# Merging the two halves of one product chain, and a later clock for stores, in a kernel with a planned order

## Chip, core and metric

The kernel runs on one core of a Trainium2 chip. The metric is the device time of one execution in microseconds (us). A core has a matrix engine (TensorE; PE in the rows, its weight loads PEld), VectorE (DVE), ScalarE (ACT), GpSimd (POOL) and SyncE (SP). Here SP issues all loads and the stores of the result, and POOL issues the stores to scratch memory.

## What is computed

For each of 8 batches, memory attention over 8 heads of 576 tokens; the heads are joined to rows of 512 values, and two feed-forward networks follow (512 to 2048 to 512 each), the first with SiLU, the second with ELU.

```python
a = softmax(phi, axis=tokens)                  # 576 tokens, 32 memory slots
k_m, v_m = a.T @ k, a.T @ v                    # per batch and head
attn = softmax(q @ k_m.T / 8)
x = (attn @ v_m) joined over heads             # 4608 x 512
h = x @ moe_w_in;  x = (h * sigmoid(h)) @ moe_w_out
h = x @ moe2_w_in; out = elu(h) @ moe2_w_out
```

## The kernel before

**Stages.** A first part, to about 84 us, runs batch 0 in an order written out by hand (`FIRST`). From there to about 718 us `plan_first` runs the end of batch 0 and batches 1 to 6 and prepares all weights; then batch 7's last product and the whole second network (9 blocks of 512 tokens) follow under a second plan. The output of the first network goes to scratch memory (`x2d`) and is read back by the second.

**Numbers as two halves.** Operands of the large products are split into a high and a low fp16 part, after a scaling by a power of two taken from a sum of squares. The weights `w_out` of the first network (`w1o`) are read as four column blocks `wB[0..3]`. Blocks e and e + 2 belong to half e (0 or 1), each half with its own scale `s_w1o[:, e]`. `plan_w1o` waits for the sums of squares of its own two blocks, forms four sums of quarters (VectorE), splits seven operands j = 0..6 (high part on ScalarE, low part on VectorE, tile `hl_q`), and stores each to scratch (`w1os[e][j]`, POOL). `plan_quads` does the same for the second network's weights (`w2is`, `w2os`): a load into the buffer `raw`, five steps of conversion into `quad`, then splits and stores. `hl_q` lies in the same two `raw` buffers, so that a load waits for an earlier store to land, and a split too.

**Seven products in place of eight.** The second matrix product of the first network is computed from seven products of quarters (`plan_out1`): product j runs 8 steps over both halves e, alternating, into the PSUM pair `ph` (one bank for each half). The results are then copied (ScalarE, `copy_of`) or added (VectorE, `add_to`) into `y`, one instruction for each half: tile `y` is 4 x 288 values for one half, in two buffers (`NY`). After that the half is stored (`x2d`, POOL), and `squares` sums its squares in place on ScalarE, for the scale of the second network. That instruction overwrites `y`, so it waits until the store has landed.

**The plan.** `Plan` is a list scheduler that runs while the program is built. Each task has an engine, an estimated cost, a rank and dependencies; tasks are issued engine by engine, each time the ready task of the lowest rank at the earliest free time. In the plan of `plan_first` the ranks come from due times (`by_due`, with `ahead` = 35 us). The engines work through the resulting order and take no notice of the estimates: where an estimate was too short, an instruction waits in its place and holds all behind it on its engine. The estimates that matter here:

```python
def load(self, kb, ...):  cost = (2.2 if self.ahead is None else 3.6) + late + kb / 350
def store(self, kb, ...): cost = 4.0 + kb / 200, of which the POOL queue is held 1.2
t = pl.store(590, r - 2500, store, ...)          # plan_out1, one for each half
... pl.add("ACT", act(4 * HS), r - 100, squares, [t])
```

A load of 1024 KB is thus put at 6.5 us, a store of 512 KB at 6.56 us and a store of 590 KB at 6.95 us.

Of the kernel before, what the change touches and what calls it, by code (L numbers as in the profile page):

```python
# [39 lines left out]
NY = 2  # L40
NT = 3
KVLATE, QLATE = 1.0, 3.0
NKV = 3
# [47 lines left out]
def attn_moe_moe(ctx: ExitStack, tc: tile.TileContext, qT, phiT, kvm, kvt, w1i, w1o, w2i, w2o, out):  # L91
# [96 lines left out]
    class Plan:  # L188
# [62 lines left out]
        def run(self):  # L251
# [44 lines left out]
    s_w1o, n_w1o, p_w1o, q_w1o = col("s_w1o", 2), col("n_w1o", 2), col("p_w1o", 2), col("q_w1o", KD * NS)  # L296
# [53 lines left out]
    def junk_tile():  # L350
        return big.tile([P, 4 * HS], F32, tag="y", name="junk", bufs=NY).bitcast(F16)

# [97 lines left out]
    def plan_pair(pl, rank, e, s_all, n_all, negative, part, store, items, deps):  # L450
# [6 lines left out]
        for i, (get, j) in enumerate(items):  # L457
            s = (n_all if j in negative else s_all)[:, e:e + 1]
# [32 lines left out]
    def plan_w1o(pl, rank, e, ready, deps):  # L491


        def get():
            m, c = small("mq1"), kept("mq4", 4)
            for k, d in enumerate((e, e + 2)):
                nc.vector.tensor_copy(c[:, 2 * k:2 * k + 2], q_w1o[:, NS * d:NS * d + NS])
            nc.vector.tensor_reduce(out=m, in_=c, axis=AX.X, op=ALU.add)
            return m

        sc = plan_scales(pl, rank, e, get, s_w1o, n_w1o, p_w1o, ready)
# [15 lines left out]
        def pair(rank, items, deps):  # L517
            read, done = plan_pair(pl, rank, e, s_w1o, n_w1o, (3,), part_out, store_out(w1os), [
                (quad.get(x) or (lambda x=x: t[x]), j) for x, j in items], deps + [sc])
# [21 lines left out]
    def plan_quads(pl, due, src, e, shape, s_all, n_all, p_all, part, store):  # L541
# [43 lines left out]
        def pair(k, items, deps):  # L585
            pl.due = due[k]
            read, _ = plan_pair(pl, 0, e, s_all, n_all, (3,), part, store, [
# [135 lines left out]
    def mem_scales(b):  # L723

        z = st[b]
        z["inv1"], z["pvw"], z["c1"], z["io1"] = (kept(x, n, 3) for x, n in (("inv1", NF), ("pvw", 1), ("c1", 1), ("io1", 2)))
# [313 lines left out]
    def y_tile(name="y"):  # L1040
        return big.tile([P, 4, HS], F32, tag="y", name=name, bufs=NY)

# [13 lines left out]
    def plan_out1_first(pl, rank, ready):  # L1056
# [14 lines left out]
        def result(d):  # L1071
            z["x", d] = y_tile("x2e").rearrange("p a s -> p (a s)")[:, :S]
            acopy(halves(z["x", d]), z[d][0])

        for d in range(KD):
# [7 lines left out]
            c = pl.add("ACT", act(S, False), rank, lambda d=d: result(d), [t] + pl.ring("y", NY))  # L1083
            free.append(c)
            xfree = pl.take("y", c)
# [98 lines left out]
    def plan_out1(pl, b, r, silus, made, stored, scales, y_tile, y_ring):  # L1184
# [6 lines left out]
        w = [dict() for _ in range(2)]  # L1191
# [14 lines left out]
        def unit(e, j, q):  # L1206
            bank, at = BANK[j]
            if bank not in ps:
                ps[bank] = ps_half(SLOT[bank])[1]
            t = z["T", WSEQ.index(j)]  # L1210
            mm3([ps[bank][e]], [slice(0, HS)], [
# [28 lines left out]
        def copy_of(e, bank, s, deps):  # L1240
            def fn():
                if "y" not in w[e]:
                    w[e]["y"] = y_tile()
# [3 lines left out]
        def add_to(e, bank, s, from_, deps):  # L1247
            return pl.add("DVE", dve(HS), r - 2500, lambda: nc.vector.scalar_tensor_tensor(
                out=w[e]["y"][:, s], in0=ps[bank][e], scalar=z["io1"][:, e:e + 1], in1=w[e]["y"][:, from_],
                op0=ALU.mult, op1=ALU.add), deps)  # L1250

        E = range(2)
        C11, C12, C21, C22 = range(4)
        p1 = product(0, [])
        yfree = []
        c1 = []
        for e in E:
            c1.append(copy_of(e, 0, C11, p1 + [io] + pl.ring(*y_ring)))
            yfree.append(pl.take(y_ring[0], c1[e]))
        p2 = product(1, [])  # L1260
        c11 = [add_to(e, 1, C11, C11, [c1[e]] + p2) for e in E]
        p6 = product(5, c1)
        u2 = [copy_of(e, 0, C21, [c1[e]] + p6) for e in E]
        p7 = product(6, c11)
        s7 = [copy_of(e, 1, C22, [c1[e]] + p7) for e in E]
        p5 = product(4, u2)
        c22 = [add_to(e, 0, C22, C22, [s7[e]] + p5) for e in E]
        p4 = product(3, s7)
        c21 = [add_to(e, 1, C21, C21, [u2[e]] + p4) for e in E]
        p3 = product(2, c22)  # L1270
        c12 = [copy_of(e, 0, C12, [c1[e]] + p3) for e in E]
        free[0] += c12
        free[1] += c21
        done = []
        for e in E:
            def store(e=e):
                nc.gpsimd.dma_start(out=x2d[b][:, e::2], in_=w[e]["y"].rearrange("p (a t) s -> p a (t s)", a=2))
# [365 lines left out]
    def plan_first():  # L1643
# [84 lines left out]
        for b in range(1, B):  # L1728
# [24 lines left out]
            plan_out1(pl, b, 1000 * b + 400, silus, 0, stored if b == 1 else {}, [A[b]["scales"]], y_tile, ("y", NY))  # L1753
# [11 lines left out]
    with tc.manual_schedule():  # L1765
# [16 lines left out]
        for n in range(NT):  # L1782
            last["T_free", n] = pl.take("T", None)
        out1, loads = plan_out1(
            pl, B - 1, 0, None, NT, {}, [], lambda: ph2.tile([P, 4, HS], F32, tag="y", name="y", bufs=2), ("y", 2))
# [8 lines left out]
        for i in range(NB):  # L1794
# [3 lines left out]
            if i == 2:  # L1798
                pl.add("DVE", 2.5, 1000 * i + RANK["x2"], lambda: x2_scales(B - 1, NB), [y[i]["t_done", KQ - 1, 0]] + out1)
# [53 lines left out]
```

## Time and profile before

| | us |
|---|---|
| median of 3 runs | 1409.9 (1408.24 to 1411.55) |
| the profiled execution | 1407.48 |
| its span on the core | 1405.5 |
| PE busy | 1354.2 |
| DVE busy | 1127.9 |
| ACT busy | 951.1 |

A row of the timeline gives the start in us from the start of the span, the duration in us, the engine, the line of the kernel, the operation, its tiles and how many were merged into the row; in brackets stands the time that the engine sat idle before it and what released it. "PEclk" is the clock that the chip granted to TensorE, as a share of its full 2.4 GHz; the other level is 1.2 GHz. Ends of matmuls are modelled, so a busy PE need not be a fast one.

### The profile page before, as it was taken

What the parts mean: (1) busy time and instruction counts of PE and PEld (TensorE: products, weight loads), DVE (VectorE), ACT (ScalarE), POOL (GpSimd) and SP (SyncE); (2) the same over time, 40 slices, a digit from 0 to 9 for tenths busy, and PEclk for the clock granted to TensorE, in tenths of its full rate; (3) what the DMA queues carried; (4) which work ended last, traced back from release to release, by engine and by line L of the source; (5) the groups of instructions that cost most, each with busy time, mean ns of one, the idle gap of its engine ahead of it and who ended that gap; (6) DMA issues with size and microseconds to landing.
All of it is one profiled execution on the core that took longest, in us unless ns stands there. A gap on an engine that the chain in (4) does not pass through costs nothing.

```text
span 1405.5 us, 28627 instructions
## 1 busy us (share of the span) xinstructions
PE 1354.2 (96%) x12048; PEld 1092.9 (78%) x12048; DVE 1127.9 (80%) x1753; ACT 951.1 (68%) x1357; POOL 51.1 (4%) x85
## 2 busy tenths in 40 slices
PE   4999999999989999999998999999999999999998
PEld 2667676776756767676786888888888888888887
DVE  6889788796977989797767787887879787878784
ACT  3667765957857596776657576767667676767583
POOL 0001100000010010011000000000000000000000
PEclk8999999999999999999999999999999999999999
DMA  9565767367475657736293233332424151514130
GB/s 363 178 227 176 287 246 255 140 218 278 150 246 197 232 188 253 257 129 224 104 369 132 83 112 107 110 109 84 135 69 151 43 177 43 163 56 136 57 120 31
DMA packets 68801, 233.06 MB, mean 166 GB/s; under 512 B 9025, under 2 KB 15169, under 8 KB 64065
## 3 DMA queue, kind: packets, MB, share of 16 engines
q1 hardware_dynamic: 60288, 199.78, 42.1%
q0 software_dynamic: 8384, 31.46, 5.6%
q8 instruction: 94, 1.54, 0.4%
q14 instruction: 35, 0.28, 0.1%
HBM read 186.12 MB, written 40.89 MB: 162 GB/s over the span
## 4 chain that ended last, share of the span: by engine, by line
PE 79%; DMA 7%; DVE 4%; issue 4%; ACT 4%; POOL 0%; SPq 0%; ACTq 0%; POOLq 0%; DVEq 0%
PE ph L1020 24%; PE o L1020 22%; PE h2A L1020 12%; PE h2D L1020 9%; PE ph L1069 4%; DMA wi<-w2is 3%; PE ph L1027 2%; PE sc L775 2%; PE up L860 2%; PE kvp L679 1%; DMA kv<-in_kvm 1%; DMA x2d<-y 1%; DMA raw<-in_w2i 1%; DMA w2is<-hl_q 1%; DVE T L175 1%
## 5 line engine op out<-in xcount | busy, mean ns | idle before, releaser
L1020 PE MATMUL o<-t,wq 128*128 128x256 f16 x3024 | 361.4, 273 | 1.3 <-DVE t L175 1.3
L1020 PEld LDWEIGHTS <-wi 128*128 128x128 f16 x3024 | 296.2, 98 | 50.1 <-issue 7.2
L1020 PEld LDWEIGHTS <-wq 128*128 128x128 f16 x3024 | 296.1, 98 | 36.3 <-issue 1.7
L1020 PE MATMUL ph<-T,w1s 128*128 128x288 f16 x2352 | 301.9, 286 | 0.0
L1020 PEld LDWEIGHTS <-w1s 128*128 128x128 f16 x2352 | 225.9, 98 | 64.7 <-issue 8.6
L1020 PE MATMUL h2A<-xh,wi 128*128 128x256 f16 x1728 | 228.2, 274 | 10.0 <-ACT h L1457 6.0
L1457 ACT ACTIVATE h<-h2A,inv 128x256 f32<-128x256 f32 x288 | 133.3, 467 | 111.7 <-PE h2A L1020 108.9
L1020 PE MATMUL ph<-aT,u 128*128 128x288 f16 x1344 | 179.8, 290 | 8.8 <-ACT h L1106 8.5
L1020 PEld LDWEIGHTS <-u 128*128 128x128 f16 x1344 | 129.0, 99 | 59.2 <-issue 26.4
L170 ACT ACTIVATE t<-h,s_g 128x768 f16<-128x768 f32 (+1 forms) x144 | 147.4, 1037 | 37.5 <-DVE h L1499 25.9
L1020 PE MATMUL h2D<-xh,wi 128*128 128x256 f16 x1296 | 172.0, 274 | 0.1
L175 DVE SCALAR_TENSOR_TENSOR t<-h,s_g,t 128x768 f16<-128x768 f32 (+1 forms) x144 | 163.4, 1145 | 4.9 <-ACT t L170 4.9
L175 DVE SCALAR_TENSOR_TENSOR T<-h,c,T 128x1152 f16<-128x1152 f32 x98 | 137.2, 1412 | 22.7 <-ACT T L170 22.6
L1461 DVE SCALAR_TENSOR_TENSOR h<-h2D,inv,h 128x256 f32<-128x256 f32 x216 | 102.4, 480 | 65.1 <-PE h2D L1020 43.8
L170 ACT ACTIVATE T<-h,c 128x1152 f16<-128x1152 f32 x98 | 119.9, 1253 | 25.1 <-DVE h L134 19.9
L134 DVE TENSOR_TENSOR h<-h 128x256 f32<-128x256 f32 (+1 forms) x302 | 128.5, 463 | 3.0
L1499 DVE SCALAR_TENSOR_TENSOR h<-e,h 128x1024 f32<-128x1024 f32 x72 | 87.9, 1221 | 20.7 <-ACT e L1495 20.2
L1106 ACT ACTIVATE h<-ph,inv 128x576 f32<-128x576 f32 x112 | 82.1, 737 | 15.9 <-PE ph L1020 15.4
L1492 ACT ACTIVATE e<-h 128x1024 f32<-128x1024 f32 x72 | 75.5, 1048 | 13.7 <-DVE h L1461 13.6
L1495 ACT ACTIVATE e<-e 128x1024 f32<-128x1024 f32 x72 | 75.7, 1051 | 1.0
L1069 PE MATMUL ph<-h,w1o 128*128 128x288 f32 x256 | 66.7, 416 | 0.0
L134 DVE TENSOR_TENSOR h<-h,h 128x1152 f32<-128x1152 f32 x42 | 56.5, 1353 | 7.2 <-ACT h L1106 7.0
(183 smaller groups left out, 1271.2 us busy)
## 6 DMA issues: line engine op xcount, KB each, us to landing
w1s<-w1os SPq DMA_DIRECT2D x98, 512.0 KB, 4.5
wi<-w2is SPq DMA_DIRECT2D x56, 896.0 KB, 4.7
kv<-in_kvm SPq DMA_DIRECT2D x48, 256.0 KB, 5.5
q<-in_qT SPq DMA_DIRECT2D x32, 288.0 KB, 7.3
out<-ye SPq DMA_DIRECT2D x36, 256.0 KB, 2.0
raw<-in_w1i SPq DMA_DIRECT2D x8, 1024.0 KB, 11.5
raw<-in_w1o SPq DMA_DIRECT2D x8, 1024.0 KB, 4.9
raw<-in_w2i SPq DMA_DIRECT2D x8, 1024.0 KB, 6.7
```

Source lines behind the costliest of these rows:

```text
L134: nc.vector.tensor_tensor(out=out, in0=a, in1=b, op=op)
L170: nc.scalar.activation(out=hi, in_=x, func=AF.Copy, scale=s)
L175: nc.vector.scalar_tensor_tensor(out=lo, in0=x, scalar=s, in1=hi, op0=ALU.mult, op1=ALU.subtract)
L775: nc.tensor.matmul(ps[o:o + 64, c // 2, 2 * p:2 * p + 2], z["q", p][:, t0:t0 + 64], z["kT"][:, p // 2, 64 * (p % 2):64 * (p % 2) + 64], st ...
L1020: nc.tensor.matmul(o, w, x[:, c], start=first, stop=last, **how)
L1069: nc.tensor.matmul(z[d][1][t], wB[d][:, k], h[k // KQ][:, t, k % KQ], start=(k == 0), stop=(k == KF - 1))
L1106: nc.scalar.activation(out=h[m // KQ][:, :, m % KQ], in_=w.pop(m), func=AF.Silu, scale=z["inv1"][:, m // 4:m // 4 + 1])
L1457: nc.scalar.activation(out=w["x"][:, s], in_=w["A"], func=AF.Copy, scale=inv)
L1461: return pl.add("DVE", COST["add"], base, lambda: nc.vector.scalar_tensor_tensor(out=w["x"][:, s], in0=w["D"], scalar=inv, in1=w["x"][:, s ...
L1492: nc.scalar.activation(out=w["e"], in_=w["x"][:, B21:], func=AF.Relu, scale=-1.0)
L1495: nc.scalar.activation(out=w["e"], in_=w["e"], func=AF.Exp, scale=-1.0)
L1499: nc.vector.scalar_tensor_tensor(out=x, in0=w["e"], scalar=-1.0, in1=x, op0=ALU.add, op1=ALU.max)
```

## The change

There are five parts. (1) One scale for the whole of `w_out`: its columns become single, and `plan_w1o` for both halves waits for one `plan_w1o_scales`, which needs the sums of squares of all four blocks. (2) `y` becomes one tile for both halves in one buffer, and `copy_of`, `add_to` and `squares` each become one instruction over both halves; the two stores remain. The first batch's `x2e` uses quarters of the same tile. (3) `squares` gets rank 0 in `plan_first` (where due times replace it) and rank 1200 for the last batch, which puts it after ScalarE's work on the second network's first block (`in2`); and the gate that opens the second network's PSUM buffers no longer waits for it. (4) In `plan_first` a store is estimated 2 us longer and a weight load into `raw` (`plan_quads`) 2 us longer. (5) There ScalarE and VectorE may stay free for up to 0.6 us, where the chosen task would end over 0.3 us after a task arrives whose rank is lower by more than 10.

```diff
-NY = 2
+RAWLATE, STORE = 2.0, 6.0
+SOON, EARLIER = 0.6, 10.0
...
-            return self.add("POOL", 4.0 + kb / 200, rank, fn, deps, 1.2)
+            return self.add("POOL", (4.0 if self.ahead is None else STORE) + kb / 200, rank, fn, deps, 1.2)
...
                     i = min((i for i in r if at[i] <= start), key=lambda i: (self.tasks[i][2], i))
+                    if self.ahead is not None and eng in ("ACT", "DVE"):
+                        rank, end = self.tasks[i][2], start + self.tasks[i][1]
+                        soon = [k for k in r if start < at[k] <= start + SOON and end > at[k] + SOON / 2 and self.tasks[k][2] < rank - EARLIER]
+                        if soon:
+                            i = min(soon, key=lambda k: (at[k], k))
+                            start = at[i]
...
-    def plan_w1o(pl, rank, e, ready, deps):
+    def plan_w1o_scales(pl, rank, ready):
         def get():
-            m, c = small("mq1"), kept("mq4", 4)
-            for k, d in enumerate((e, e + 2)):
-                nc.vector.tensor_copy(c[:, 2 * k:2 * k + 2], q_w1o[:, NS * d:NS * d + NS])
-            nc.vector.tensor_reduce(out=m, in_=c, axis=AX.X, op=ALU.add)
+            m = small("mq1")
+            nc.vector.tensor_reduce(out=m, in_=q_w1o, axis=AX.X, op=ALU.add)
             return m
-        sc = plan_scales(pl, rank, e, get, s_w1o, n_w1o, p_w1o, ready)
+        return plan_scales(pl, rank, 0, get, s_w1o, n_w1o, p_w1o, ready)
+
+    def plan_w1o(pl, rank, e, sc):
...
-            load = pl.load(1024, 0, lambda k=k: load64(src, e, k), pl.ring("raw", 2))
+            load = pl.load(1024, 0, lambda k=k: load64(src, e, k), pl.ring("raw", 2), RAWLATE)
...
-        return big.tile([P, 4, HS], F32, tag="y", name=name, bufs=NY)
+        return big.tile([P, 2, 4, HS], F32, tag="y", name=name)
...
-        def copy_of(e, bank, s, deps):
+        def copy_of(bank, s, deps):
...
-                acopy(w[e]["y"][:, s], ps[bank][e], z["io1"][:, e:e + 1])
-            return pl.add("ACT", act(HS), r - 2500, fn, deps)
+                acopy(w["y"][:, :, s], ps[bank], z["io1"])
+            return pl.add("ACT", act(S), r - 2500, fn, deps)
...
-            def squares(e=e):
-                sumsq(mx_x2[:, b, e:e + 1], w[e]["y"], w[e]["y"])
-            t = pl.store(590, r - 2500, store, [c11[e], c12[e], c21[e], c22[e]])
-            yfree[e].append(pl.add("ACT", act(4 * HS), r - 100, squares, [t]))
-            done += [yfree[e][-1], c12[e], c21[e], p3[e]]
-        return done, [loads[j][0] for j in WSEQ]
+        def squares():
+            x = w["y"].rearrange("p e a s -> p (e a s)")
+            sumsq(mx_x2[:, b, 0:1], x, x)
+        t = [pl.store(590, r - 2500, lambda e=e: store(e), [c11, c12, c21, c22]) for e in range(2)]
+        yfree.append(pl.add("ACT", act(8 * HS), squares_rank, squares, t))
+        return p3 + [c12, c21], yfree[-1:], [loads[j][0] for j in WSEQ]
...
+        sc = plan_w1o_scales(pl, 260, sum(sq.values(), []))
         for e in range(2):
-            t, r = plan_w1o(pl, 260 + 20 * e, e, sq[e] + sq[e + 2], [])
+            t, r = plan_w1o(pl, 260 + 20 * e, e, sc)
...
-            pl, B - 1, 0, None, NT, {}, [], lambda: ph2.tile([P, 4, HS], F32, tag="y", name="y", bufs=2), ("y", 2))
+            pl, B - 1, 0, None, NT, {}, [], lambda: ph2.tile([P, 2, 4, HS], F32, tag="y", name="y"), ("y", 1), 1200)
```

## Rows read from the trace of the kernel before

**Rows 1.** Page, engines: busy us, share of the span, instructions.

```profile
PE 1354.2 (96%) x12048; PEld 1092.9 (78%) x12048; DVE 1127.9 (80%) x1753; ACT 951.1 (68%) x1357; POOL 51.1 (4%) x85
```

**Rows 2.** Windows: PE, PEld, DVE, ACT, POOL busy; clock; DMA; GB/s.

```profile
158.00:681.00 523.00, 511.22 (x4775) 373.27 (x4776) 429.64 (x583) 370.72 (x537) 38.75 (x57) 0.99 0.61 214
...
718.00:1405.50 687.50, 671.40 (x6083) 595.38 (x6080) 538.99 (x908) 467.64 (x653) 1.80 (x3) 1.00 0.33 108
```

**Rows 3.** Waits of PE over the span: total, times, longest us.

```profile
PE ph L1020 <- ACT h L1106: 8.5, 6, 4.3
PE h2A L1020 <- ACT h L1457: 6.0, 5, 3.9
```

**Rows 4.** Windows around four stalls of PE, columns as in rows 2.

```profile
100.00:116.00 16.00, 12.93 (x115) 9.31 (x104) 13.71 (x23) 9.32 (x19) 1.22 (x1) 0.89 0.86 254
328.00:350.00 22.00, 18.59 (x160) 12.11 (x159) 14.67 (x16) 15.79 (x24) 0.00 (x0) 0.92 0.75 271
400.00:433.00 33.00, 28.69 (x249) 18.14 (x248) 20.90 (x24) 22.47 (x32) 5.69 (x8) 0.90 0.70 235
736.00:772.00 36.00, 29.36 (x230) 23.81 (x228) 26.17 (x44) 26.77 (x38) 0.00 (x0) 0.91 0.43 151
```

**Rows 5.** Chain of waits, 310 to 331: start us, us, what.

```profile
310.27 2.48 DVE hl_q L175 x2
...
317.64 7.22 DMA w2is<-hl_q
325.05 6.19 DMA raw<-in_w2i
```

**Rows 6.** Timeline 331 to 334, with the idle time before.

```profile
331.27 1.12 ACT L311 ACTIVATE quad<-raw 128x1024 f32<-128x1024 f32 x1 [3.11 <-DMA raw<-in_w2i]
...
333.07 4.77 PE L1020 MATMUL ph<-aT,u 128*128 128x288 f16 x24 [2.02 <-ACT h L1106]
```

**Rows 7.** Timeline 399 to 418, the second stall of that kind.

```profile
399.87 1.28 DVE L175 SCALAR_TENSOR_TENSOR hl_q<-quad,s_w2i,hl_q 128x1024 f16<-128x1024 f32 x1
...
406.67 0.72 POOL L448 DMA_DIRECT2D w2is<-hl_q  x1 [5.30 <-issue]
...
415.57 1.15 ACT L170 ACTIVATE hl_q<-quad,s_w2i 128x1024 f16<-128x1024 f32 x1 [4.23 <-DMA w2is<-hl_q]
...
417.40 3.04 PE L1020 MATMUL ph<-aT,u 128*128 128x288 f16 x12 [4.27 <-ACT h L1106]
```

**Rows 8.** Timeline 729 to 744, the last batch's stores and squares.

```profile
729.45 1.43 POOL L1277 DMA_DIRECT2D x2d<-y  x2 [41.01 <-ACT y L178]
...
738.75 1.16 ACT L354 ACTIVATE y<-y 128x1152 f32<-128x1152 f32 x1 [3.00 <-DMA x2d<-y]
...
741.38 1.16 ACT L354 ACTIVATE y<-y 128x1152 f32<-128x1152 f32 x1 [1.38 <-DMA x2d<-y]
...
743.41 1.44 PE L1020 MATMUL h2A<-xh,wi 128*128 128x256 f16 x6 [3.88 <-ACT h L1457]
```

**Rows 9.** Lines by form: count, busy us, mean ns; copies, adds, SiLU.

```profile
L178 ACT ACTIVATE y<-ph,io 128x288 f32<-128x288 f32 x56 | 24.9, 495 | 29.7 <-PE ph L1020 28.2 <-DVE io L735 1.4
...
L1248 DVE SCALAR_TENSOR_TENSOR y<-ph,io,y 128x288 f32<-128x288 f32 x42 | 19.8, 509 | 2.7 <-PE ph L1020 2.6
...
L1106 ACT ACTIVATE h<-ph,inv 128x576 f32<-128x576 f32 x112 | 82.1, 737 | 15.9 <-PE ph L1020 15.4
```

**Rows 10.** Timeline at 150: the second scale of w_out is done.

```profile
150.19 0.15 DVE L488 TENSOR_SCALAR n_w1o<-s_w1o 128x1 f32<-128x1 f32 x1
```

**Rows 11.** DVE in the next 75 us, columns as in rows 2.

```profile
150.00:175.00 25.00, 25.00 (x220) 17.52 (x220) 19.30 (x19) 19.96 (x28) 4.29 (x8) 1.00 0.87 305
175.00:200.00 25.00, 25.00 (x222) 18.72 (x221) 21.44 (x20) 19.44 (x26) 0.53 (x1) 1.00 0.76 271
```

**Rows 12.** DMA issues: count, KB, median us to landing.

```profile
w1os<-hl_q POOLq DMA_DIRECT2D x14, 512.0 KB, 4.8
w2is<-hl_q POOLq DMA_DIRECT2D x14, 512.0 KB, 5.2
```

More of the change, by code (lines that the diff above doesn't have):

```diff
@@ L448, in store_in, with plan_pair @@
         nc.gpsimd.dma_start(out=w2is[e][:, :, j], in_=hl.rearrange("p (q c) -> p q c", q=4))
-    def plan_pair(pl, rank, e, s_all, n_all, negative, part, store, items, deps):
+    def plan_pair(pl, rank, e, s_all, n_all, negative, part, store, c, items, deps):
         z = {}
@@ L517, in pair @@
         def pair(rank, items, deps):
-            read, done = plan_pair(pl, rank, e, s_w1o, n_w1o, (3,), part_out, store_out(w1os), [
+            read, done = plan_pair(pl, rank, e, s_w1o, n_w1o, (3,), part_out, store_out(w1os), 0, [
                 (quad.get(x) or (lambda x=x: t[x]), j) for x, j in items], deps + [sc])
@@ L586, in pair @@
             pl.due = due[k]
-            read, _ = plan_pair(pl, 0, e, s_all, n_all, (3,), part, store, [
+            read, _ = plan_pair(pl, 0, e, s_all, n_all, (3,), part, store, e, [
                 (lambda x=x: t[x], j) for x, j in items], deps)
@@ L1082, in plan_out1_first @@
                 done[d, q] = t
-            c = pl.add("ACT", act(S, False), rank, lambda d=d: result(d), [t] + pl.ring("y", NY))
+            c = pl.add("ACT", act(S, False), rank, lambda d=d: result(d), [t] + (pl.ring("y", 1) if d == 0 else [done["y"]]))
             free.append(c)
-            xfree = pl.take("y", c)
+            if d == 0:
+                done["y"] = c
+                xfree = pl.take("y", c)
             t = pl.store(295, rank, lambda d=d: nc.gpsimd.dma_start(out=x2d[0][:, d], in_=z["x", d]), [c])
@@ L1182, in plan_w1s, with plan_out1 @@
         return t
-    def plan_out1(pl, b, r, silus, made, stored, scales, y_tile, y_ring):
+    def plan_out1(pl, b, r, silus, made, stored, scales, y_tile, y_ring, squares_rank=0):
         z = st[b]
-        w = [dict() for _ in range(2)]
+        w = {}
         ps = {}
@@ L1238, in product @@
             return [units(j, e, q, deps) for q in range(KQ) for e in range(2)][-2:]
-        def copy_of(e, bank, s, deps):
+        def copy_of(bank, s, deps):
             def fn():
-                if "y" not in w[e]:
-                    w[e]["y"] = y_tile()
-                acopy(w[e]["y"][:, s], ps[bank][e], z["io1"][:, e:e + 1])
-            return pl.add("ACT", act(HS), r - 2500, fn, deps)
-        def add_to(e, bank, s, from_, deps):
-            return pl.add("DVE", dve(HS), r - 2500, lambda: nc.vector.scalar_tensor_tensor(
-                out=w[e]["y"][:, s], in0=ps[bank][e], scalar=z["io1"][:, e:e + 1], in1=w[e]["y"][:, from_],
+                if "y" not in w:
+                    w["y"] = y_tile()
+                acopy(w["y"][:, :, s], ps[bank], z["io1"])
+            return pl.add("ACT", act(S), r - 2500, fn, deps)
@@ L1250, in add_to @@
+        def add_to(bank, s, from_, deps):
+            return pl.add("DVE", dve(S), r - 2500, lambda: nc.vector.scalar_tensor_tensor(
+                out=w["y"][:, :, s], in0=ps[bank], scalar=z["io1"], in1=w["y"][:, :, from_],
                 op0=ALU.mult, op1=ALU.add), deps)
-        E = range(2)
         C11, C12, C21, C22 = range(4)
         p1 = product(0, [])
[L1255 to L1259, printed above, removed]
@@ L1260, in plan_out1 @@
-        p2 = product(1, [])
[L1261 to L1271, printed above, removed]
@@ L1285, in plan_out1 @@
-        return done, [loads[j][0] for j in WSEQ]
+        c1 = copy_of(0, C11, p1 + [io] + pl.ring(*y_ring))
+        yfree = pl.take(y_ring[0], c1)
+        p2 = product(1, [])
+        c11 = add_to(1, C11, C11, [c1] + p2)
+        p6 = product(5, [c1])
+        u2 = copy_of(0, C21, [c1] + p6)
+        p7 = product(6, [c11])
+        s7 = copy_of(1, C22, [c1] + p7)
+        p5 = product(4, [u2])
+        c22 = add_to(0, C22, C22, [s7] + p5)
+        p4 = product(3, [s7])
+        c21 = add_to(1, C21, C21, [u2] + p4)
@@ new lines, in plan_out1, with store @@
+        p3 = product(2, [c22])
+        c12 = copy_of(0, C12, [c1] + p3)
+        free[0].append(c12)
+        free[1].append(c21)
+        def store(e):
+            nc.gpsimd.dma_start(out=x2d[b][:, e::2], in_=w["y"][:, e].rearrange("p (a t) s -> p a (t s)", a=2))
+        def squares():
[3 more added lines that the diff above has]
+        yfree.append(pl.add("ACT", act(8 * HS), squares_rank, squares, t))
@@ L1752, in plan_first @@
             U[b + 1] = plan_u(pl, b + 1, 1000 * b + 150, mem[b + 1], ready)
-            plan_out1(pl, b, 1000 * b + 400, silus, 0, stored if b == 1 else {}, [A[b]["scales"]], y_tile, ("y", NY))
+            plan_out1(pl, b, 1000 * b + 400, silus, 0, stored if b == 1 else {}, [A[b]["scales"]], y_tile, ("y", 1))
         n = 2
@@ L1783, in attn_moe_moe @@
             last["T_free", n] = pl.take("T", None)
[L1784 to L1785 removed]
+        out1, squares, loads = plan_out1(
+            pl, B - 1, 0, None, NT, {}, [], lambda: ph2.tile([P, 2, 4, HS], F32, tag="y", name="y"), ("y", 1), 1200)
         w1s_load = pl.gates["x"] = loads[4:5]
@@ L1798, in attn_moe_moe @@
             if i == 2:
-                pl.add("DVE", 2.5, 1000 * i + RANK["x2"], lambda: x2_scales(B - 1, NB), [y[i]["t_done", KQ - 1, 0]] + out1)
+                pl.add("DVE", 2.5, 1000 * i + RANK["x2"], lambda: x2_scales(B - 1, NB), [y[i]["t_done", KQ - 1, 0]] + squares)
             if i + 1 < NB:
```

22 lines of the change are left out of this document (9 added, 13 removed).

## The prediction

> **What bounds the kernel now.** Start with the page's list of engines: TensorE is busy for 96% of the span, VectorE for 80%, ScalarE for 68% [rows 1]. TensorE is the bound, and no part of the change takes a matmul away. So an instruction saved on ScalarE or VectorE is worth nothing by itself; what can be won is time in which TensorE stands still, or runs at the lower of its two clocks (1.2 for 2.4 GHz) after it stood still. Next come windows by stage: in the planned stage from 158 to 681 TensorE lacks 523 - 511.2 = 11.8 us, in the last one, from 718 on, 687.5 - 671.4 = 16.1 us [rows 2]. Then the waits of TensorE. The two large entries behind the opening are waits for ScalarE: 8.5 us for SiLU results of the first network (L1106) and 6.0 us for copies of the second (L1457) [rows 3]. ScalarE is idle for a third of the time, so these are not a lack of throughput: something stood ahead of the needed instruction. Windows around the places show what one such stall costs. The reader takes two things from each row: window less busy time, and one less the granted clock, times the window. At 328 that is 3.4 + 1.8 = 5.2 us, at 400 it is 4.3 + 3.3 = 7.6 us, at 736 it is 6.6 + 3.2 = 9.9 us, at 100 it is 3.1 + 1.8 = 4.8 us [rows 4]. The clock's share falls partly into the idle time, so these are upper ends.
>
> The chain of waits tells what stood ahead at 328. VectorE has finished the low part of a w2 operand at 310.27 + 2.48 = 312.75; the store that frees the buffer starts at 317.64 and lands at 324.86; the next weight load then takes 6.19 us [rows 5]. ScalarE waits 3.11 us for this load, with the SiLU that TensorE needs queued behind, and TensorE loses 2.02 us at once [rows 6]. The 24 matmuls after it take 4.77 us. The plan had put that store at 4.0 + 512/200 = 6.56 us; from data to landing it took 12.1, so it was 5.5 us late. The load was put at 6.5 us and took 6.2: it was not late by itself. At 415 it is the same with a store alone. Data are ready at 399.87 + 1.28 = 401.15, POOL cannot issue before 406.67 although it sits idle for 5.30 us, and ScalarE gets the buffer at 415.57, after an idle 4.23 us; TensorE then stands for 4.27 us [rows 7]. The third place is the change of networks: the last batch's stores are issued at 729.45, the squares of `y` wait for them, 3.00 and then 1.38 us, and TensorE stands for 3.88 us because the copies of the second network are queued behind [rows 8].
>
> **Part by part.**
>
> *Squares of the last batch (rank 1200).* In the old plan they had the lowest rank of all, so they went ahead of every copy as soon as the stores were thought landed (6.95 us). Now they come after ScalarE's work on the first block. The plan still fills a gap: if ScalarE is free and nothing else is ready, the squares go in, and may still wait. They now wait for both stores at once, the second of which let ScalarE go at 741.38 [rows 8]. Bounds: all of the 9.9 us of the place; or, if the gap comes at once, nothing. Below nothing too: one instruction over 2304 values takes about 2 x 1.16 = 2.3 us in one piece (estimate from rows 8), during which no copy can pass, so +2. I take -6, nearest to the wait itself (3.88) and its share of clock: at least most of the 4.4 us that ScalarE idled goes, since the copies that were ready then come first.
>
> *Stores and loads in `raw` planned 2 us later.* At 328 the chain of store and load gets 4 us more where it was 5.5 us late; the 3.11 us of waiting on ScalarE should be gone. I take the whole place, -5.2. At 400 only the store is in the chain: 2 of 4.23 us go, so I take 2.0/4.23 of 7.6 = -3.6. Together -8.8, rounded to -8 since the clock's share is an upper end. Bounds: 0 (the tasks that move into the space wait in their turn) and -12.8 (both places whole). Loads and stores that follow on SP and POOL are also issued later; their cover is that the plan works 35 us ahead of TensorE. Where that cover is gone, the price is a stall like the one at 100.
>
> A rule of the Trainium skill speaks against this part: "DMA: Bandwidth & Descriptors", section on the anatomy of one DMA on the GpSimd path, gives about 2.0 us plus the bytes at 436 GB/s, which for 512 KB is an estimate of 3.2 us. By it 6.56 us was ample already, and the sum would lose the -8. The rows differ: 4.8 and 5.2 us are the medians from issue to landing [rows 12], and the store of rows 5 took 7.2 us and waited 4.9 us for its issue.
>
> *One instruction for both halves.* 28 copies replace 56 and 21 adds replace 42. The copies go from 24.9 us of ScalarE to 28 x 0.737 (SiLU over the same 576 values) = 20.6; the adds cost 19.8 us now, and I leave VectorE's gain at about 2.5 (between 0 and half) [rows 9]. No product starts later, since it waited for both halves before. Nearly all of this lies beside TensorE's work. Only at the end of a batch does TensorE wait for a freed bank; there the pair is some 0.15 us shorter, seven times: -0.5 taken, bounds 0 and -2. The single buffer of `y` costs nothing: in the old form a half also waited for its own squares of the batch before, and these have most of a batch of room (seven batches lie between 158 and 718, 80 us each).
>
> *One scale for w_out.* Half 1's scale was there at 150.19 [rows 10]; the common one needs the same last sum of squares, so it comes then too. Half 0's work, done before that time until now, moves behind it: seven low parts of 1.28 us and four sums of the same shape, 11 x 1.28 = 14.1 us of VectorE, and 7 x 1.15 = 8 us of ScalarE [rows 7]. From 150 to 200 VectorE is idle for 50 - 19.3 - 21.4 = 9.3 us [rows 11], so 4.8 us do not fit and push other work. TensorE is busy for the full 50 us there, and the plan has 35 us in hand; that is the cover, and I take 0. Bounds: 0 and, with the cover gone, +14.1, plus 1.8 for the clock. Queued behind on POOL: the fourteen stores of 4.8 us median [rows 12] now come together, and behind them on SP the loads of these operands.
>
> *Waiting for urgent tasks.* A wait of up to 0.6 us puts a SiLU or a copy ahead of a split of 1.15 to 1.28 us. If the urgent task is late, the engine idles for nothing; VectorE is 82% busy from 158 to 681 [rows 2]. Everything behind 84 us is ordered anew by this and the other parts, and a new order has stalls of its own which no row of this trace can place. The nearest row is the stall at 100, where ScalarE waits for a load that was planned as it is now: 4.8 us [rows 4]. I take +4 for it all, between -5 (that stall goes, and none comes) and +10 (two such).
>
> **Sum.** -6 - 8 - 0.5 + 0 + 4 = -10.5 us. The profiled execution took 1407.5 us with a span of 1405.5, so it would come to 1397.0; it lies 2.4 us below the median of 1409.9, and on the median's scale I predict 1399.4.
>
> **Rivals.**
>
> (1) *The late stores stay late.* POOL waits with an idle engine for a store ahead of it (5.30 us in rows 7); the delay comes from the queue, not from the estimate, so a store behind another remains 3 to 5 us late and ScalarE waits elsewhere. For it: of fourteen stores most were within 6.56 us at the median, and still two pairs stalled. The rule of the Trainium skill on the page named above would end here too. Then -6 - 0.5 + 4 and -1 of the -8: 1406.4; without new stalls 1402.4. I put it at 1404. Chance 0.2.
>
> (2) *The squares only change their gap.* ScalarE has small gaps in the first block, the plan puts the 2.3 us into the first one past its 6.95 us, and the landing is just as late. Then the -6 shrinks to -1, and the sum is -5.5: 1404.4. Chance 0.12.
>
> (3) *Slower: the common scale of w_out.* Place: 150 to 230, the first use of the stored operands. VectorE's 14.1 us and the fourteen stores in a row hold the first products' weights, and TensorE waits for them in an order that cannot be changed any more. At the whole price of 15.9 us, with -6 - 8 - 0.5 + 4 beside it, the time is 1415.3. It decides the sign from the point where more than 10.5 us of the 15.9 land on TensorE. Against it: TensorE is busy throughout there, and the due times rank these splits first. Chance 0.13, with other slow new orders.
>
> (4) *No effect in sum*: gains and new stalls cancel, within 0.2% of 1409.9. Chance 0.1, beside the forecast's 0.45.
>
> **Range and chances.** A measurement of this kernel can tell about 0.2% (2.8 us) from no change. The forecast's own range, by the bounds, is 1390 to 1404; rivals 1 and 2 reach to 1406, the cancelled case to 1412, and only the slow case beyond that, with some of the forecast's lower end, is left out: 1390 to 1412. Faster: 0.45 + 0.18 + 0.1 = 0.73; within 0.2%: 0.1 + 0.04 = 0.14; slower: 0.13.
>
> **What would show it.** In the changed profile: no wait of ScalarE for `x2d<-y` with TensorE idle behind it, around 740, and the window there with a clock near 1.00; the squares as 7 instructions of about 2.1 us; 28 copies near 0.74 us; no wait of ScalarE for `raw<-in_w2i` or `w2is<-hl_q` over 2 us; half 0's stores of w_out after 150 and no wait of TensorE between 150 and 240. The prediction is wrong if stalls of TensorE on L1106 in the planned stage add up to as much as the 8.5 us of now, if the first use of `w1s` waits for a load, or if TensorE's stall at the change of networks stays above 3 us.

## Result: faster by 1.3%, and the profile after

The changed kernel takes 1391.0 us (median of 4 runs, 1390.5 to 1392.2), the kernel before beside it 1409.5. The ratio is 0.9869 with a 95% interval of 0.9852 to 0.9886: 18.5 us less, between 16 and 21. The prediction was 1399.4 with a range of 1390 to 1412. The direction and the range held; the size was 10.5 us by the forecast and is 18.5 by the medians, or 16.5 between the two profiled executions (1407.48 and 1390.94), whose spans are 1405.5 and 1389.2 us. One execution of a later kernel (the urgent wait limited to 0.5 us) took 5309 us for a reason that its record does not show, and is in no ratio below.

The page's engine line answers [rows 1]:

```profile
PE 1345.7 (97%) x12048; PEld 1089.7 (78%) x12048; DVE 1122.9 (81%) x1721; ACT 943.9 (68%) x1315; POOL 52.8 (4%) x84
```

TensorE has the same 12048 matmuls and is busy 1354.2 - 1345.7 = 8.5 us less. Equal work that takes less time is clock, and the mean granted clock, 0.989 before and 0.995 now, says the same: the share that is missing to 1 is worth about 15.5 us of the one span and 6.9 of the other. The rest of the 16.3 us of span, 7.8, is idle time that went. So about half of what these stalls cost lay in the lower clock that followed them.

Windows of the changed kernel at the places of [rows 4] (columns as there; the last one is moved by the 11 us that were won by then):

```profile
100.00:116.00 16.00, 12.85 (x122) 9.40 (x111) 12.03 (x18) 7.32 (x12) 0.35 (x1) 0.89 0.96 282
328.00:350.00 22.00, 21.84 (x202) 15.24 (x201) 16.66 (x17) 18.86 (x26) 0.00 (x0) 1.00 0.70 262
400.00:433.00 33.00, 32.31 (x298) 21.85 (x297) 27.01 (x29) 29.30 (x38) 5.68 (x8) 1.00 0.72 245
725.00:761.00 36.00, 32.64 (x286) 27.38 (x284) 30.44 (x50) 31.58 (x44) 0.00 (x0) 1.00 0.50 174
```

Idle time plus lost clock was 5.2, 7.6 and 9.9 us at the last three; it is 0.2, 0.7 and 3.4 now, all at full clock. The place at 100 stayed as it was (4.9 for 4.8). TensorE's waits over the span, answering [rows 3] (total, times, longest):

```profile
PE h2A L1029 <- DMA wi<-w2is: 6.9, 9, 2.0
...
PE kvTp L753 <- ACT pad L179: 4.1, 3, 3.2
PE ph L1029 <- ACT h L1119: 3.3, 7, 0.9
PE h2A L1029 <- ACT h L1466: 1.8, 5, 0.6
PE kvp L688 <- ACT quad L319: 1.5, 1, 1.5
```

The waits for SiLU results fell from 8.5 to 3.3 us and those for the second network's copies from 6.0 to 1.8. One wait grew: loads of `wi` in the second network, which were 3.4 us in all before. It looks like a price of the third place's cure, though no run tests that alone: in the six kernels of this document without a long stall at the change of networks these loads cost TensorE 5.0 to 7.0 us, in the eight that have one (2.9 us or more) 1.5 to 4.2.

Where the time came from can be read off the first store of `y` of each batch, a mark that stands in both traces. Before, for batches 2, 3 and 4 (the last batch's stands in [rows 8]):

```profile
318.44 0.67 POOL L1277 DMA_DIRECT2D x2d<-y  x1
...
407.31 0.78 POOL L1277 DMA_DIRECT2D x2d<-y  x1
415.78 0.68 POOL L1277 DMA_DIRECT2D x2d<-y  x1 [7.69 <-issue]
...
491.69 1.40 POOL L1277 DMA_DIRECT2D x2d<-y  x2 [18.47 <-DVE aT L175]
```

And after, with the last batch's:

```profile
317.73 0.67 POOL L1286 DMA_DIRECT2D x2d<-y  x1 [2.22 <-ACT y L179]
...
403.48 0.78 POOL L1286 DMA_DIRECT2D x2d<-y  x1
410.62 0.68 POOL L1286 DMA_DIRECT2D x2d<-y  x1 [6.36 <-issue]
...
481.45 1.40 POOL L1286 DMA_DIRECT2D x2d<-y  x2 [18.93 <-ACT y L179]
...
717.99 1.43 POOL L1286 DMA_DIRECT2D x2d<-y  x2 [40.89 <-ACT h L1466]
```

Up to 318 the gain is 0.7 us. The stretch with the place at 328 gives 3.1, the one with the place at 400 gives 6.4, the rest of the planned stage 1.2 (11.46 in all at 718), and all from there to the end 4.8. These are single executions. Two kernels of the experiments show how far the marks move by themselves, since up to the change of networks they run in the order of one of these two. The kernel before with its last squares late has the four marks at 321.81, 411.03, 493.21 and 731.17, the changed kernel with its squares first at 318.63, 405.06, 482.97 and 719.52. So the gain at 328 lies between 2.4 and 3.5 us, the one at 400 between 4.2 and 6.5, and the 0.7 up to 318 is not clear of chance.

### The profile page after: what moved, and what is told of

Read it like the earlier page. It is cut to its first block, busy times and chain, and to the rows that moved or that the text cites. A ratio compares the mean times of both kernels' runs of the same rounds, so it can differ in the third digit from the quotient of the medians.

```text
span 1389.2 us, 28545 instructions
## 1 busy us (share of the span) xinstructions
PE 1345.7 (97%) x12048; PEld 1089.7 (78%) x12048; DVE 1122.9 (81%) x1721; ACT 943.9 (68%) x1315; POOL 52.8 (4%) x84
## 4 chain that ended last, share of the span: by engine, by line
PE 78%; DMA 7%; ACT 6%; DVE 5%; issue 4%; POOL 0%; SPq 0%; ACTq 0%; POOLq 0%; DVEq 0%
PE ph L1029 27%; PE o L1029 22%; PE h2A L1029 12%; PE h2D L1029 9%; DMA wi<-w2is 4%; PE ph L1036 2%; PE up L869 2%; PE sc L784 1%; PE ph L1078 1%; PE kvp L688 1%; DMA raw<-in_w1o 1%; DMA kv<-in_kvm 1%; ACT h L1119 1%; DMA w1os<-hl_q 1%; ACT y L362 1%
## 5 line engine op out<-in xcount | busy, mean ns | idle before, releaser
L1029 PEld LDWEIGHTS <-wi 128*128 128x128 f16 x3024 | 294.6, 98 | 48.8 <-DMA wi<-w2is 10.7
L1029 PE MATMUL ph<-aT,u 128*128 128x288 f16 x1344 | 175.7, 287 | 3.6 <-ACT h L1119 3.3
L176 DVE SCALAR_TENSOR_TENSOR u<-up,u 128x512 f16<-128x512 f32 x56 | 38.4, 686 | 31.2 <-ACT u L171 31.0
```

What stands on the lines that cost most here:

```text
L176: nc.vector.scalar_tensor_tensor(out=lo, in0=x, scalar=s, in1=hi, op0=ALU.mult, op1=ALU.subtract)
L1029: nc.tensor.matmul(o, w, x[:, c], start=first, stop=last, **how)
```

## Experiments

Each result is a ratio to the kernel before, run on the same chip; differences in us are ratios times 1409. Tables of TensorE's waits leave out the first 90 to 100 us.

**Parts one by one, on the kernel before.** First the squares of the last batch alone:

```diff
-        done += [yfree[e][-1], c12[e], c21[e], p3[e]]
+        sq.append(yfree[e][-1])
+        done += [c12[e], c21[e], p3[e]]
...
-        pl.add("ACT", act(4 * HS), r - 100, squares, [t])
+        pl.add("ACT", act(4 * HS), r - 100 if squares_rank is None else squares_rank, squares, [t])
```

> The kernel before with one edit: the last batch's squares of y get rank 1200 and are no longer in the gate of the second network. Theory (the stall at 740 is the squares alone): everything up to 718 us is the same instruction by instruction, TensorE's stall of 3.88 us and the clock's dip there go, and the time falls by 4 to 7 us, to 1402 to 1406 (the term of the prediction was 6). Rival (the squares only change their gap): ScalarE still waits over 2 us for the stores with copies behind it, and the time falls by less than 2 us.

Measured: 0.9982 (0.9964 to 1.0000), 2.5 us less with an interval down to 0, which leaves room for both theories. The timeline decides (ScalarE's row and TensorE's):

```profile
741.17 1.16 ACT L354 ACTIVATE y<-y 128x1152 f32<-128x1152 f32 x1 [3.70 <-DMA x2d<-y]
...
744.15 0.82 PE L1020 MATMUL h2A<-xh,wi 128*128 128x256 f16 x6 [2.93 <-ACT h L1458]
```

Rival 2 of the prediction is what this kernel does: the first half's squares went into ScalarE's next gap, 6.3 us after the store's issue at 731.17, and waited 3.70 us there, with the copies queued behind. The second half's squares moved far enough to wait for nothing. The dip of the clock is gone (1.00 from 738 to 774), the stall is not. The late rank by itself is half a cure.

Then the later stores and loads alone (the `load`, `store` and `RAWLATE` lines of the diff):

```diff
+RAWLATE, STORE = 2.0, 6.0
-            return self.add("POOL", 4.0 + kb / 200, rank, fn, deps, 1.2)
+            return self.add("POOL", (4.0 if self.ahead is None else STORE) + kb / 200, rank, fn, deps, 1.2)
```

> The kernel before with one edit: stores of the planned stage are put at 6.0 instead of 4.0 us plus size, loads of w2 at 2.0 us more. Theory (the plan's short estimate made the stalls at 328 and 400): both stalls of TensorE go, and the time falls by 8 to 10 us (term of the prediction 8; the changed kernel's trace shows 9.2 us gained between 317 and 482). Rival 1 (the delay is the queue's, late stores stay late): ScalarE waits elsewhere for the same buffers, and the gain is 0 to 2 us. Third theory (the urgent-task rule did it): no gain either, and the run with that rule alone gets it.

Measured: 1.0005 (0.9990 to 1.0019). No gain, although the waits it aimed at are gone: ScalarE's waits for loads and stores of the second network's weights fell from 11.5 us to 0.2, and TensorE's for SiLU results from 8.5 to 1.9. TensorE's waits:

```profile
PE kvp L680 <- DMA kv<-in_kvm: 7.2, 3, 3.1
PE h2A L1021 <- ACT h L1458: 7.1, 5, 4.9
PE aTp L828 <- DVE att L135: 5.3, 2, 4.6
...
PE ph L1021 <- ACT h L1107: 1.9, 4, 0.6
```

The rows around the first of them, of SP's queue, POOL, ScalarE and TensorE:

```profile
325.21 1.05 SPq L638 DMA_DIRECT2D q<-in_qT  x1
332.70 0.33 SPq L306 DMA_DIRECT2D raw<-in_w2i  x1
332.83 0.68 POOL L1278 DMA_DIRECT2D x2d<-y  x1 [7.20 <-ACT h L1107]
333.08 0.42 SPq L623 DMA_DIRECT2D kv<-in_kvm  x1
...
342.42 1.16 ACT L355 ACTIVATE y<-y 128x1152 f32<-128x1152 f32 x1 [4.41 <-DMA x2d<-y]
343.58 0.72 ACT L1107 ACTIVATE h<-ph,inv 128x576 f32<-128x576 f32 x1
343.93 0.43 PE L680 MATMUL kvp<-kv,es 128*32 128x128 f32 x8 [3.05 <-DMA kv<-in_kvm]
```

SP stands from 326.3 to 332.7 at the load into `raw`, whose buffer a late store still holds. The load of `kv` is queued behind it and is issued only then, and TensorE stops for it. But SP stood as long at this load in the kernel before (from 319.0 to 325.1), and there TensorE did not wait for the `kv` load behind it. And ScalarE waits too, only no longer for `raw`: POOL, idle for 7.20 us, issues the second store of `y` 8.0 us after the first, the squares of that half wait 4.41 us for it to land, and SiLU is queued behind them. That SiLU ends at 344.30, and TensorE's next product starts at 344.35; by the order of the rows it had to wait for it, so without the late `kv` TensorE would have stood nearly as long. This is rival 1: a store behind another stays late, and ScalarE waits for it in another place (9.8 us in all for stores of `y`, 5.2 before).

The marks say where the gain went. The first stores of `y` come at 324.85, 410.25, 493.03 and 732.53, so the stretch with the place at 328 is 3.5 us shorter than before, as in the changed kernel, and the one with the place at 400 is not clearly shorter (82.8 us, against 84.4 and 82.2 in the two executions of the old order). But the first mark is 3 to 6 us later than theirs, with a new stall of 4.56 at 135 for VectorE's `att`, and the squares at the change of networks cost TensorE 4.9 us in place of 3.9. These belong to the new order.

The wait for urgent tasks alone (the six lines added in `run`):

```diff
+                    if self.ahead is not None and eng in ("ACT", "DVE"):
+                        rank, end = self.tasks[i][2], start + self.tasks[i][1]
+                        soon = [k for k in r if start < at[k] <= start + SOON and end > at[k] + SOON / 2 and self.tasks[k][2] < rank - EARLIER]
+                        if soon:
+                            i = min(soon, key=lambda k: (at[k], k))
+                            start = at[i]
```

> The kernel before with one edit: in the plan ScalarE and VectorE may wait up to 0.6 us for a task that is due more than 10 us earlier. Theory (a new order with stalls of its own, no gain of its own): between 4 us slower and 2 us faster, with the stalls at 328 and 400 still there in some place. Rival (this rule took the stalls away, since TensorE stood for SiLU results of ScalarE): 6 to 10 us faster, with the ScalarE waits for buffers in raw as long as before.

Measured: 0.9975 (0.9958 to 0.9992), 3.5 us less, between the two theories. TensorE's waits:

```profile
PE h2A L1028 <- ACT h L1465: 7.1, 5, 4.9
PE ph L1028 <- ACT h L1114: 4.3, 3, 2.5
PE aTp L835 <- DVE att L135: 3.5, 2, 3.0
```

Half of the SiLU waits went (the stall at 400 is gone, the one at 328 stands, with 2.5 and 1.7 us at 337 and 347), a new wait came, the squares stayed.

One scale alone, and one scale with merged instructions (the changed kernel with its three edits to the plan undone):

> The kernel before with one edit: one scale for both halves of w_out. Theory (rival 3 of the prediction in small: fourteen splits and stores come closer together, and stores put at 4.0 us come too late for the buffer of the next pair): ScalarE waits 2 to 4 us for a store of w_out near 185 with TensorE standing behind it, 2 to 5 us slower than before. Second theory (the 8 us of the run with merged instructions and one scale are the merged instructions' order): within 1 us of before up to 240 us and in sum. Prediction's own term: 0.

> The changed kernel with its three edits to the plan undone (stores at 4.0 us, no wait for urgent tasks, squares of the last batch first again): one scale of w_out and one instruction for both halves stay. Theory (these parts lie beside TensorE's work): 0 to 2 us faster than before, the three stalls of before still there or moved. Rival (the shorter copies and adds, or the new order that they bring, carry the 8 us by which the prediction fell short): 4 to 8 us faster.

The edit of the first, in short:

```diff
-            t, r = plan_w1o(pl, 260 + 20 * e, e, sq[e] + sq[e + 2], [])
+            t, r = plan_w1o(pl, 260 + 20 * e, e, sc)
```

Measured: 1.0016 (0.9999 to 1.0033) for the scale, 1.0060 (1.0040 to 1.0079) with the merging: 2.3 us slower with an interval that just reaches no change, and 8.5. The first theory of the scale fits, both theories of the merging had the wrong sign. Both kernels show a stall near the place that rival 3 named, by another way than it said: TensorE waits not for the stored weights, but for SiLU. One scale:

```profile
182.43 1.15 ACT L170 ACTIVATE hl_q<-quad,s_w1o 128x1024 f16<-128x1024 f32 x1 [2.72 <-DMA w1os<-hl_q]
...
184.26 1.63 PE L1021 MATMUL ph<-aT,u 128*128 128x288 f16 x12 [1.92 <-ACT h L1107]
```

With the merging:

```profile
185.18 1.15 ACT L170 ACTIVATE hl_q<-quad,s_w1o 128x1024 f16<-128x1024 f32 x1 [3.24 <-DMA w1os<-hl_q]
...
187.01 3.28 PE L1021 MATMUL ph<-aT,u 128*128 128x288 f16 x17 [2.45 <-ACT h L1111]
```

The last split of `w_out` needs the buffer of a store that is still on its way, and SiLU stands behind the split. Of the second kernel's other stalls the longest are 5.2 us at 107 (3.1 at 104 before), 4.9 on a `kv` load at 444, and 6.0 at the change of networks (3.9 before), where the merged squares wait; the long stalls at 333 and 417 are not in it. How these come to the other 6 us is not shown.

**Parts taken out of the changed kernel.** Without the wait for urgent tasks, with the stores and loads at their old times, and with the squares first:

> The changed kernel without the rule that lets ScalarE and VectorE wait for urgent tasks; all else stays. Theory I (the parts need each other: each alone gave 3 us or less, the whole 18): the stalls on late stores stay away, but others come, on SiLU, kv loads or operands of VectorE, 5 to 10 us of them, and the time is 1396 to 1402. Theory P (the parts add up, the rule is worth what it gave alone, 3 us): 1394. Theory L (the small total of stalls in the changed kernel is one lucky order among many): any single edit of the plan, this one too, brings 8 us or more: over 1399.

> The changed kernel with stores at 4.0 us plus size and no added time for loads of w2; all else stays. Theory I: ScalarE waits for buffers in raw again (at 185 for the stores of w_out as in the run with the merged instructions alone, 3.24 us there, and at the places near 330 and 410), 6 to 12 us in sum: 1397 to 1403. Theory P (alone this edit gave nothing): 1391, no difference. Theory L: over 1399.

> The changed kernel with the last batch's squares first again and in the gate of the second network; all else stays, and up to 717 us nothing differs. Theory I (rank and merging act together: alone the late rank left a wait of 3.70 us, the merged squares put early one of about 6 us): ScalarE waits 5 to 6 us for both stores, TensorE stands 5 us or more with a clock dip: 8 to 10 us longer, 1399 to 1401. Theory P (the term of the run with the late rank alone, 3.4 us): 1394 to 1395.

```diff
-RAWLATE, STORE = 2.0, 6.0
+RAWLATE, STORE = 0.0, 4.0
...
-            ... name="y"), ("y", 1), 1200)
+            ... name="y"), ("y", 1), -100)
```

(The first of these two edits is that of the second kernel, the second that of the third, which also has the squares in the gate again; the first kernel lacks the six lines shown above.) Measured: 0.9945 (0.9920 to 0.9970), 0.9910 (0.9878 to 0.9943) and 0.9921 (0.9894 to 0.9947), against 0.9869 of the whole. By differences of the ratios the parts are worth 10.7, 5.8 and 7.3 us in company, where they gave 3.5, -0.7 and 2.5 alone. The interval of the second touches that of the whole, and its profiled execution (1392.0 us) is only 1 us longer than the changed kernel's, so that part's worth is not shown. The other two are clear of it. The medians were 1402.1, 1395.4 and 1399.3 us: the first lies at the upper end of theory I and fits theory L too, the second falls between theories I and P, the third is theory I's. TensorE's waits without the urgent rule:

```profile
PE ph L1021 <- ACT h L1111: 6.0, 11, 1.6
PE kvp L680 <- DMA kv<-in_kvm: 3.5, 2, 2.5
PE up L861 <- DVE vT L175: 1.8, 1, 1.8
PE up L861 <- DVE u L175: 1.6, 2, 1.5
```

No single stall is long, but 11 small ones wait for SiLU results where the changed kernel has 7 of little over half that sum. With the old store times the waits for late loads are back, on ScalarE:

```profile
ACT quad L319 <- DMA raw<-in_w2o: 3.5, 2, 3.0
ACT quad L319 <- DMA raw<-in_w2i: 3.4, 2, 2.1
```

TensorE in that kernel loses 6.0 us to three waits for `kv`, the longest 3.7. No ScalarE wait near 185 comes back, against what theory I said. With the squares first, ScalarE's row is:

```profile
731.96 2.12 ACT L362 ACTIVATE y<-y 128x2304 f32<-128x2304 f32 x1 [4.34 <-DMA x2d<-y]
```

Its stores were issued at 719.52. The instruction stood ready from 727.62, 8.1 us later, and got its data 12.4 us after the issue. TensorE stands 5.73 us behind it. In the changed kernel the same instruction comes 12.9 us after the issue and waits for nothing, with 0.4 us to spare if the stores took as long to land:

```profile
730.85 2.11 ACT L362 ACTIVATE y<-y 128x2304 f32<-128x2304 f32 x1
```

So the cure of the third place has two parts: the rank, and one instruction that needs both stores, which the plan puts into a later gap than it put the first half's. Up to 718 the two kernels run in one order, and from there to the end this one takes 5.5 us longer; the other 1.5 between the two spans had come before and are chance.

**Is it a lucky order?** Neighbours of two of the numbers, and the plan's three edits without merging and scale:

> The changed kernel with the urgent wait limited to 0.5 instead of 0.6 us; the order of instructions is the same up to some 320 us and another one from there. Theory M (the long stalls are gone by the parts together, and small stalls of 1 to 2 us are what any order has): 1389 to 1396, no stall of TensorE over 3 us behind 160. Theory L (the changed kernel has a lucky order): a stall of 3 us or more comes somewhere behind 320, and the time is 1396 to 1402.

> The changed kernel with stores put at 7.0 instead of 6.0 us plus size, a new order from the start. Theory M: 1389 to 1396, with no ScalarE wait for a store in raw or for y over 2 us. Theory L: 1396 to 1405, with stalls of 3 us or more in new places.

> The changed kernel with the urgent wait allowed up to 0.8 instead of 0.6 us, a new order from the start. Theory M: 1389 to 1396. Theory L: 1396 to 1405, with stalls of 3 us or more in new places.

> The kernel before with the three edits of the plan together (stores and loads later, urgent wait, squares of the last batch late), without the merged instructions and with a scale for each half of w_out. Theory I (the merged instructions are needed for the change of networks, where two squares of a half each leave a wait of 3.7 us, but not for the planned stage): no ScalarE wait for raw over 2 us up to 718, ScalarE still waits 3 us or more for a store of y near 735, 1395 to 1400. Theory P (the parts add): 1409.1 - 3.4 + 0 - 3.1 = 1402.6. Rival (the whole gain is the plan's, merging adds nothing): 1391 to 1393.

```diff
-SOON, EARLIER = 0.6, 10.0
+SOON, EARLIER = 0.5, 10.0
...
-RAWLATE, STORE = 2.0, 6.0
+RAWLATE, STORE = 2.0, 7.0
...
-SOON, EARLIER = 0.6, 10.0
+SOON, EARLIER = 0.8, 10.0
```

Measured: 0.9874 (0.9858 to 0.9891) for 0.5; 0.9882 (0.9868 to 0.9897) for stores at 7.0; 0.9930 (0.9907 to 0.9952) for 0.8; 0.9934 (0.9912 to 0.9956) for the plan's edits alone. Two other orders are as fast as the changed kernel, so its time is not one lucky draw. A third gives 8.6 us back, and not by stalls of 3 us or more:

```profile
PE kvp L688 <- DMA kv<-in_kvm: 2.9, 2, 2.8
...
PE ph L1029 <- ACT y L179: 2.2, 1, 2.2
PE up L869 <- DVE u L176: 1.8, 2, 1.5
PE o L1029 <- DVE t L176: 1.5, 2, 1.3
```

The stalls of 2.8 us at 573 (`kv`) and 2.2 at 689 (`y`) lie where the time is lost: from batch 5's first store of `y` to the last batch's (562.38 to 726.20) this kernel takes 163.8 us, the changed one 153.4, and the clock from 562 to 600 is 0.95. So theory M holds for two of the three and neither theory for the last; some 8 us is what one order may differ from a neighbour. That also limits the single parts: 5.8 and 10.7 us for parts that reorder everything behind 84 us are of the size that 0.2 us in one limit moved, so the part and the order that came with it are not told apart. The squares are, since there the orders agree up to 718. The plan's edits alone, 9.3 us faster, leave ScalarE 4.01 us at a store of `y` at 730, as theory I said, with TensorE's longest wait for it 3.2; one wait for `raw` of 2.3 us is left too, where it said none over 2. None of the neighbours beats the changed kernel.

## Why the prediction was right, and by how much it was off

*What bounds the kernel, and the three places: right.* All three are gone, and the stretches that hold them give 3.1 + 6.4 + 4.8 of the 16.3 us between the profiles.

*Squares of the last batch, -6: nearly right in size, for half the reason.* The stretch from 718 on gives 4.8, though waits for `wi` grew by 3.5 us in it. The prediction took the rank for the cure and the merged instruction for a risk (+2). Rank alone left 3.70 us of waiting, the merged squares put first wait 4.34; only both together have none. The sign that was named held: no ScalarE wait for `x2d<-y` with TensorE idle behind, and a clock of 1.00.

*Stores and loads later, -8: the places gave 9.5, the part alone nothing.* The working took 5.2 at 328 and 3.6 at 400; the stretches gave 3.1 and 6.4, with all parts together. The step "the 3.11 us of waiting on ScalarE should be gone" held, and what was built on it, "I take the whole place, -5.2", did not hold for this edit: alone it left TensorE 3.05 us of waiting at that place, for a `kv` load behind the load of `raw` and for SiLU behind a late store of `y`, and lost elsewhere what it won. That is the bound of 0 that the working gave, "the tasks that move into the space wait in their turn". The prediction had named the load queue and put its cover at 35 us; for `kv` the cover was not there. The rule of the Trainium skill ("DMA: Bandwidth & Descriptors", section on the anatomy of one DMA on the GpSimd path), by which the old 6.56 us was ample, is not borne out by the rows: with the old times of stores and loads in the changed kernel ScalarE waits 6.9 us for loads into `raw`. What the prediction drew from it, that the sum would lose the -8, is what this part alone measured, but not for that reason. What it leaves out here is the wait for the issue: POOL still idles 6.36 us ahead of one store of the changed kernel (410.62), as it did 7.69 before (415.78).

*Merged instructions, -0.5: the durations right, the worth not.* Rows of the changed kernel by form, answering [rows 9]:

```profile
L179 ACT ACTIVATE y<-ph,io 128x576 f32<-128x576 f32 x28 | 20.6, 737 | 31.7 <-PE ph L1029 30.3 <-DVE io L744 1.4
...
L362 ACT ACTIVATE y<-y 128x2304 f32<-128x2304 f32 x7 | 14.8, 2116 | 0.6 <-DMA x2d<-y 0.6
...
L1262 DVE SCALAR_TENSOR_TENSOR y<-ph,io,y 128x576 f32<-128x576 f32 x21 | 16.9, 804 | 2.9 <-PE ph L1029 2.7
```

The copies took the 20.6 us that were predicted. The adds take 2.9 us less, against 2.5 taken. Yet the merging and the scale together are worth +8.5 us alone and about -9.2 in the company of the plan's edits (0.9934 to 0.9869). They have no price of their own, and no run parts the merging from the scale in that company.

*One scale, 0: right in the sum, wrong on the time.* The step "the common one needs the same last sum of squares, so it comes then too", at 150, failed. In the changed kernel VectorE's rows are:

```profile
127.87 0.16 DVE L503 TENSOR_REDUCE mq<-q_w1o 128x1 f32<-128x8 f32 x1 [3.21 <-ACT junk_o L362]
...
130.97 0.15 DVE L167 TENSOR_SCALAR s_w1o<-rec 128x1 f32<-128x1 f32 x1
```

Before, half 0's scale was there at 124 and half 1's at 150, and I took the latter for the time at which the last sum of squares was known. It was the time at which half 1's rank let VectorE get to it: ScalarE had all eight sums by 124. The common scale costs half 0 only 7 us and gives half 1 some 19. The stores of `w_out` begin at 135.32 and end at 180.86, before at 131.76 and 177.34. So the prediction's sign "half 0's stores of w_out after 150" did not come. A part of rival 3 did exist, stores of `w_out` that come too close together: 2.7 to 3.2 us of waiting on ScalarE at 185 where the scale was tried on the old order. But it held up SiLU, and no product waited for its weights. In the changed kernel that wait is 0.92 us, and it does not come back with the old store times, so it is the order that covers it, not the later stores.

*New order, +4: the term that failed.* Its bounds were -5 and +10, by the stall at 100. That stall stayed, and everything outside the three stretches came to 0.7 + 1.2 = 1.9 us gained, where this term and the -0.5 had 3.5 us lost. The difference, 5.4 us, is nearly all of the 6 by which the forecast fell short between the profiles; the errors of the other two terms (+1.2 and -1.5) cancel. With the marks of the other two executions the 1.9 lies between 1 and 5.5, so the term's sign is what failed, and its size is known to a few us only. For single parts the worry was sound: the late stores alone brought 12.5 us of waits for `kv` and `att`. What the prediction did not see is that the wait for urgent tasks may go against such stalls. It entered this part as a cost, and without it the changed kernel is 10.7 us slower, the largest of the three differences, though their intervals overlap and an order alone can move 8.6.

*The sum.* It came out near because the terms were read at the places of the old stalls, and all the parts together did clear these. As a sum over edits it was wrong: alone the parts gain 3.5 + 2.5 - 0.7 - 8.5 = -3.2 us, which is a loss, where the whole gains 18.5.

*The range* held with 1 us to spare at its lower end, and in part by luck. Its 1390 is not the sum of the bounds given part by part, which is -9.9 - 12.8 - 2 - 5 = -29.7, or 1380 on the median's scale.

*The other signs* held: no ScalarE wait for `raw<-in_w2i` at all and one of 1.1 us for `w2is<-hl_q`, a single TensorE wait over half a microsecond between 150 and 240 (0.60), and no stall over 1.46 us at the change of networks.

*Left open.* Why an urgent wait of 0.8 us gives back 8.6 us where 0.5 and 0.6 do not was followed no further than to its two stalls and the clock behind them. And no run tells the urgent rule's own effect on small stalls from that of the order which it happens to give with the other parts.

## What to carry to other kernels

Price a planner's edits by the stalls they clear, but expect the sum of single tests to mislead: measure the set, and each part left out of it. When a wait for a late buffer is planned away on one engine, look at who else is queued behind the same stores (here the load queue, with another load behind it, and ScalarE's next wait, for a store of `y`). Before a part gets a price from one run, run a neighbour of its numbers: here 0.2 us in one limit moved 8.6. A time in a trace at which something was computed is not the time at which it could have been: look for the last input's row.

## What the chip showed beside this

A stall of TensorE cost about as much again in clock: of 16.3 us of span, 8.5 were the same matmuls at full clock. Two stores of 590 KB, issued back to back on POOL, let ScalarE go 12.4 us after the first issue (the kernel with the squares first), while 512 KB stores had a median of 4.8 and 5.2 [rows 12]. The fourteen stores of `y` took 8.8 us at the median, in both kernels:

```profile
x2d<-y POOLq DMA_DIRECT2D x14, 576.0 KB, 8.8
```

The old plan put them at 6.95 us; `plan_first` puts them at 8.95 now. A copy over 576 values takes 737 ns and one over 288 takes 495, so one instruction saves 253 ns over two; the squares over 2304 values take 2116 ns where two over 1152 took 2 x 1161.
